# Later Down products, an earlier cast, and the first cuts of w2 on ScalarE and GpSimd

## The chip, the cores and the metric

The kernel runs on one core of a Trainium2 chip. The metric is the device time of one execution in microseconds. The engines are TensorE (PE; its weight loads are shown apart as PEld), VectorE (DVE), ScalarE (ACT), GpSimd (POOL) and SyncE (SP), which issues the transfers.

## The reference

The input x is 2048 tokens by 512, with 32 heads of 16 and an FFN of width 1792. All values are float32.

```python
xn = layernorm(x)
q, k, v = (xn @ wqkv) split in three, 32 heads
scores = q @ k.T * Dh**-0.5, masked to 0 <= i - j < 256
s = softmax(scores) @ v, heads joined, @ wo
h = silu(x @ w1) * (x @ w3)
g = silu(h @ w2)
out = x + s * g
```

Only the FFN's weights w1, w3 and w2 and its products are touched by the change.

## The kernel before, in words

The tokens are cut into four tiles of 512 (t = 0 to 3). Attention works on a tile in groups of heads; the FFN works on a tile in 14 blocks f of 128 columns of w1 and w3 (rows of w2). Everything is multiplied in float16 in two halves: a value is scaled by a power of two, its rounding to float16 is the upper half, what is left over is the lower half, and a product is three matmuls (upper times upper, upper times lower, lower times upper).

**Where the halves of a weight come from.** A weight block arrives as float32. Its squares are summed (`measure` at L249 for w1 and w3, `measure_down` at L941 for w2), the sums are cast to bfloat16 (`sb`, at L945 for w2), a tiny matmul (L285) adds them over partitions, and a chain of small VectorE instructions (L294 to L304, then L956 to L966) turns them into a scale `sw`. Then the block is cut. There are two ways to cut: `split` scales and rounds on ScalarE (L333) and subtracts on VectorE (L334); `split_pool` scales in place on ScalarE (L342), rounds on ScalarE (L343), and subtracts on GpSimd in four pieces of 128 columns (L345). w2 is measured and scaled in four groups of blocks, 0 to 3, 4 to 7, 8 to 10 and 11 to 13. Before the change group 0 is cut by `split`, the others by `split_pool`.

**The FFN.** `gate_up(t, f)` makes 24 matmuls into two PSUM banks (L1058): gate in one, up in the other. ScalarE takes the tanh of gate (L1073), VectorE forms the product out of the gate bank (L1077) and then the product with up (L1082), and so empties the banks; ScalarE casts the result (L1091) and GpSimd subtracts for the lower half (L339). There are two such banks, which take turns: whoever writes a bank next waits until its last reader is done. `down(t, k, b)` multiplies the blocks of group k with w2 for 128 tokens (L1283) into a bank of the same pair, and VectorE adds it to an accumulator (L1304 for group 0, L1307 for the others).

**Attention beside it.** For each unit of heads, a first pass writes scores (L671) into the tensor `s` or `po` and VectorE takes their maximum (L685); a second pass writes scores again (L759) into `s`, VectorE adds the mask (L766), ScalarE takes the exponential (L769), and L787 multiplies with the values into `po`. `s` has two buffers and `po` one. `project` is another user of the two banks (L601), with a ScalarE cast (L618) and a VectorE subtraction (L622). The turned x goes through `s` or `po` as well (L515), with L524 and L525 on VectorE.

**What sets the order.** TensorE's order is written out by hand: attention's steps take pieces from the list that `feed_forward` returns, so many matmuls per step. `later(n, work)` puts work off by n such steps. On the other engines a list scheduler orders by priority and by the estimated readiness; `urgent()` raises the priority, and `behind_exp()` or `tc.issue_after(...)` only fix that something is issued behind a given instruction.

Of the kernel before, what the change touches and what calls it, by code (L numbers as in the profile page):

```python
# [23 lines left out]
D = 512  # L24
# [59 lines left out]
def tile_block(ctx: ExitStack, tc: tile.TileContext, x, wqkv, wo, w1, w3, w2, out):  # L84
# [147 lines left out]
    def behind_exp():  # L232

        return tc.issue_after(lasts["exp"].ins) if "exp" in lasts else nullcontext()
# [97 lines left out]
    def split(hi, lo, raw, s):  # L332
        lasts["hi"] = nc.scalar.activation(hi, raw, AF.Copy, scale=s)  # L333
        lasts["cut"] = nc.vector.scalar_tensor_tensor(lo, raw, s, hi, op0=ALU.mult, op1=ALU.subtract)  # L334
# [6 lines left out]
    def split_pool(hi, lo, raw, s):  # L341
        nc.scalar.activation(raw, raw, AF.Copy, scale=s)  # L342
        nc.scalar.copy(hi, raw)  # L343
        for c in range(0, 512, P):
            nc.gpsimd.tensor_sub(lo[:, c:c + P], raw[:, c:c + P], hi[:, c:c + P])  # L345
# [587 lines left out]
    def measure_down(k, f):  # L933

        f0, f1 = GROUPS[k]
        n = f1 - f0
        if f == f0:
            NORMS[k] = small.tile([P, n], F32, name="ssq2")
        sq = ppool.tile([P, D], BF16, name="sqa", bufs=1)
        with behind_exp():  # L940
            nc.scalar.activation(sq, RAW2[f], AF.Square, accum_out=NORMS[k][:, f - f0:f - f0 + 1])  # L941
        if f < f1 - 1:
            return
        sb = small.tile([P, n], BF16, name="sb2")
        nc.vector.tensor_copy(sb, NORMS[k])  # L945

        def scale(s):
            p2 = small.tile([P, n], F32, name="pp2")
            def bound():
                with tc.issue_after(lasts["emptied"].ins):  # L950
                    rest(p2)
            return then(s, powers(sb, n, p2, None, s), lambda: later(1, bound))

        def rest(p2):
            assert measured >= set(range(f0, f1))
            nc.vector.tensor_mul(p2, p2, p13[:, f0:f1])  # L956
            q = small.tile([P, 1], F32, name="q")
            nc.vector.tensor_reduce(q, p2, axis=AX.X, op=ALU.max)
            nc.vector.tensor_scalar(down_scale[:, k:k + 1], q, 1.0 / (HS * WS), None, op0=ALU.mult)
            if k:  # L960
                nc.vector.tensor_max(fold_q, fold_q, q)
            else:
                nc.vector.tensor_copy(fold_q, q)
            nc.vector.reciprocal(q, q)
            sw = small.tile([P, 4], F32, name="sw2")
            nc.vector.tensor_scalar(sw[:, 0:n], p13[:, f0:f1], q, WS, op0=ALU.mult, op1=ALU.mult)  # L966

            def cut(f):
                raw = RAW2.pop(f)
                WF.setdefault((0, f), [[None, None], None])[1] = b = take(F16)  # L970
                if k == 0:
                    with tc.issue_after(lasts["emptied"].ins):
                        split(b[:, 0:D], b[:, D:], raw, sw[:, f - f0:f - f0 + 1])
                else:
                    with behind_exp():
                        split_pool(b[:, 0:D], b[:, D:], raw, sw[:, f - f0:f - f0 + 1])
                give(raw, after=5)
            for i, f in enumerate(range(f0, f1)):
                later(1 + 2 * i, lambda f=f: cut(f))
            if f1 == FB:  # L980
                later(4, fold_scales)
        beside_scores(2, scale)
# [394 lines left out]
    def feed_forward():  # L1377

        pieces = []
        late = []  # L1380
        cuts_at = []
        for t in range(NT):
            for f in range(FB):
                if t == 0:

                    if (f % 2 or f == 0) and f + LEAD < FB - 2:
                        pieces += [(0, lambda f=f: load(0, f)) for f in (range(f + LEAD, f + LEAD + 2) if f else range(4, LEAD + 1))]
                    elif f + LEAD == FB - 1:
                        pieces += [(0, lambda f=f: load(0, f)) for f in range(FB - 2, FB)]
                    if f % 2 and f + 3 < FB:  # L1390
                        pieces.append((0, lambda f=f + 3: later(8, lambda: measure(f, 1, 6)) if f == 6 else measure(f, 1)))
                    pieces += [(0, lambda f=f: load_down(0, f)) for f in range(f + 2 if f else 0, min(f + 3, FB))]
                    for m in range(f + 1 if f else 0, min(f + 2, FB)):
                        k = next(k for k, (_, f1) in enumerate(GROUPS) if m < f1)
                        pieces.append((0, lambda k=k, m=m: later(2, lambda: measure_down(k, m))))
                else:
                    if f == 0:
                        pieces += [(0, lambda t=t, f=f: load(t, f)) for f in range(2)]
                    if f + 2 < FB:
                        pieces.append((0, lambda t=t, f=f + 2: load(t, f)))  # L1400

                    if t == 1:
                        pieces.append((0, lambda t=t, f=f: load_down(t, f)))
                    if t == 1 and f in FOLD_AT:
                        work = fold_weights(FOLD_AT.index(f))
                        pieces.append((0, work[0]))
                        cuts_at.append((f + 2, work))
                    for at, work in cuts_at:
                        if t == 1 and f == at:
                            pieces.append((0, work[1]))  # L1410
                if f == FB - 4 and t + 2 < NT:
                    first, second = prepare_beside(t + 2, 8)
                    pieces += first
                if f == 0 and t > 2:
                    pieces += soon
                made = gate_up(t, f)
                for at, work in cuts_at:
                    if t == 1 and f == at:
                        made.insert(2, (0, lambda work=work: later(6, work[2])))
                pieces += made  # L1420
                pieces += late
                late = []
                if t < 2:
                    for k, (f0, f1) in enumerate(GROUPS):
                        if f == f1 - 1:
                            late = [q for b in range(4) for q in down(t, k, b)]
                for k, (j0, j1) in enumerate(FOLDS):
                    if t > 1 and f == 2 * j1 - 1:
                        soon, late = folds(t, k)
                        if k == 0 or t == NT - 1:  # L1430
                            pieces += soon
            if t + 2 < NT:
                pieces.append((0, second))
        return pieces + late
# [264 lines left out]
```

## Time and profile before

| | |
|---|---|
| median of three runs | 805.73 us (805.66 to 805.86) |
| the profiled execution | 805.44 us |
| its span | 803.7 us |
| TensorE busy | 791.4 us (98% of the span) |
| VectorE, ScalarE, GpSimd busy | 624.2, 393.0, 382.1 us |

The profile is taken from one execution. Busy times are of the whole span; a row of a timeline gives the start, the duration, the engine and line, the tile written and the tiles read, how many alike instructions were joined into the row, and in brackets for how long the engine had sat idle before it and whose work ended that. A bracket on TensorE is time in which no matmul was recorded as running. Rows named m are the two shared PSUM banks, s and po attention's, slot the shared SBUF buffers.

### The profile page before, as it was taken

Reading aid. Unit: us, or ns where it says so; the run is one execution under the profiler, and the core shown is the slowest. Engines: PE = TensorE matmul, PEld = TensorE weight load, DVE = VectorE, ACT = ScalarE, POOL = GpSimd, SP = SyncE. Lnnn points to the kernel's source line nnn. Section 1 sums busy time; section 2 is a strip of 40 time slices with the busy share of each in tenths; the row PEclk is TensorE's granted clock in tenths of the full one; section 3 lists DMA queues with packets and bytes.
Section 4 is the critical chain, followed back from the end, with each engine's and each line's share of the span. In section 5 each row is a group of like instructions: output and inputs, shape, how many; then the busy total and the mean of one; then the engine's idle time right before and its main releaser. Section 6 shows DMA issues by size and latency. Waiting matters only on the chain.

```text
span 803.7 us, 23972 instructions
## 1 busy us (share of the span) xinstructions
PE 791.4 (98%) x9181; PEld 404.3 (50%) x9181; DVE 624.2 (78%) x2005; ACT 393.0 (49%) x592; POOL 382.1 (48%) x746
## 2 busy tenths in 40 slices
PE   8999999999999999999999999999999999999997
PEld 4444444444554444444445444466544754466465
DVE  8887887888898678887888888777768876874537
ACT  6988685754455544345343344344444234444411
POOL 2355467552429445365443546330446276650770
PEclk9999999999999999999999999999999999999999
DMA  9887654836665564667555733665463553334431
GB/s 283 238 261 239 187 179 117 286 98 205 188 214 188 158 221 131 216 153 250 137 195 157 226 119 102 167 177 162 132 164 85 160 155 112 89 114 136 128 97 53
DMA packets 109858, 134.18 MB, mean 167 GB/s; under 512 B 18928, under 2 KB 64944, under 8 KB 109744
## 3 DMA queue, kind: packets, MB, share of 16 engines
q1 hardware_dynamic: 109456, 132.13, 55.3%
q8 instruction: 72, 1.18, 0.6%
q10 hardware_dynamic: 288, 0.52, 0.2%
q14 instruction: 42, 0.34, 0.1%
HBM read 91.23 MB, written 36.57 MB: 159 GB/s over the span
## 4 chain that ended last, share of the span: by engine, by line
PE 82%; DVE 6%; ACT 4%; DMA 3%; issue 2%; SPq 1%; POOL 0%; DVEq 0%; ACTq 0%; POOLq 0%
PE m L1058 30%; PE po L787 9%; PE m L601 9%; PE m L1283 8%; PE m L1201 7%; PE s L759 5%; PE m L1335 4%; PE m L567 4%; PE s L671 3%; PE po L671 2%; DVE junk L685 2%; ACT pt L769 1%; DMA dW<-slot 1%; ACT slot L342 1%; DVE s L766 1%
## 5 line engine op out<-in xcount | busy, mean ns | idle before, releaser
L1058 PE MATMUL m<-XH,slot 128*128 128x512 f16 x896 | 267.3, 380 | 1.2 <-DVE slot L622 0.8
L769 ACT ACTIVATE pt<-s,es 128x1024 f32<-128x1024 f32 x152 | 167.6, 1112 | 184.4 <-DVE s L766 180.4
L1058 PEld LDWEIGHTS <-slot 128*128 128x128 f16 x1344 | 125.0, 98 | 155.1 <-issue 12.5
L1058 PE MATMUL m<-XL,slot 128*128 128x512 f16 x448 | 169.8, 379 | 0.0
L766 DVE TENSOR_TENSOR s<-s,MK 128x256 f32<-128x256 f32 (+2 forms) x280 | 118.9, 435 | 53.6 <-PE s L759 48.2
L685 DVE CUSTOM_DVE_ANT_0 junk<-s,MW 128x320 bf16<-128x320 f32 x276 | 134.1, 486 | 18.7 <-PE s L671 10.6
L339 POOL TENSOR_TENSOR slot<-slot,slot 128x256 f16<-128x256 f32 (+1 forms) x86 | 57.6, 693 | 119.5 <-DVE slot L1339 54.3
L345 POOL TENSOR_TENSOR slot<-slot,slot 128x128 f16<-128x128 f32 x168 | 68.6, 442 | 73.5 <-ACT slot L343 68.2
L685 DVE CUSTOM_DVE_ANT_0 junk<-po,MW 128x320 bf16<-128x320 f32 x172 | 83.5, 486 | 5.3 <-DVE M L685 0.5
L1283 PE MATMUL m<-slot,slot 128*128 128x512 f16 x336 | 78.5, 380 | 0.3 <-DVE slot L1077 0.2
L787 PE MATMUL po<-pt,V 64*32 64x320 f32 (+4 forms) x2880 | 77.2, 342 | 0.8 <-DVE XL L525 0.8
L601 PE MATMUL m<-XH,slot 128*128 128x512 f16 x240 | 70.8, 380 | 0.4 <-DVE slot L1077 0.4
L1201 PE MATMUL m<-slot,slot 128*128 128x256 f16 x588 | 68.4, 273 | 0.1
L1073 ACT ACTIVATE slot<-m,sgs 128x512 f32<-128x512 f32 x56 | 38.3, 684 | 54.7 <-PE m L1058 54.1
L1116 POOL TENSOR_TENSOR slot<-slot,slot 128x256 f16<-128x256 f32 x98 | 64.5, 670 | 1.1
L787 PEld LDWEIGHTS po<-pt,V 64*32 64x32 f32 x2880 | 50.7, 106 | 22.6 <-PE s L515 0.9
L1201 PEld LDWEIGHTS <-slot 128*128 128x128 f16 x588 | 56.2, 98 | 11.6 <-issue 3.0
L1077 DVE SCALAR_TENSOR_TENSOR slot<-slot,m 128x512 f32<-128x512 f32 x56 | 38.3, 684 | 27.4 <-ACT slot L1073 27.4
L759 PE MATMUL s<-qa,KA 50*64 50x320 f16 (+3 forms) x1472 | 58.3, 259 | 0.1
L601 PEld LDWEIGHTS <-slot 128*128 128x128 f16 x392 | 36.5, 98 | 42.5 <-issue 1.9
L759 PEld LDWEIGHTS <-KA 50*64 50x64 f16 x1472 | 30.1, 105 | 51.9 <-issue 32.2
L1283 PEld LDWEIGHTS <-slot 128*128 128x128 f16 x336 | 30.7, 98 | 38.7 <-issue 4.3
(191 smaller groups left out, 1134.7 us busy)
## 6 DMA issues: line engine op xcount, KB each, us to landing
slot<-dW SPq DMA_DIRECT2D x98, 256.0 KB
slot<-in_B_w_dram SPq DMA_DIRECT2D x56, 256.0 KB
slot<-dFold SPq DMA_DIRECT2D x48, 256.0 KB
dW<-slot SPq DMA_DIRECT2D x42, 256.0 KB
slot<-in_A_x_dram SPq DMA_DIRECT2D x30, 256.0 KB
KA<-dK SPq DMA_DIRECT2D x24, 288.0 KB
slot<-dWQ SPq DMA_DIRECT2D x24, 256.0 KB
qa<-dQ SPq DMA_DIRECT2D x30, 192.0 KB
```

The source lines that it names most:

```text
L339: op(out[:, c], a[:, c], b[:, c])
L345: nc.gpsimd.tensor_sub(lo[:, c:c + P], raw[:, c:c + P], hi[:, c:c + P])
L601: nc.tensor.matmul(cell["pp"][:, cols[n]], w[:, (a * NC + c) * P:(a * NC + c + 1) * P], b[:, c, cols[n]], start=n == 0 and (c, i) == parts ...
L685: lasts["maximum"] = nc.vector.tensor_tensor_reduce(out=junk[:, :n], in0=s[:, r, :n], in1=mask, scale=1.0, scalar=NEG, op0=ALU.add, op1=AL ...
L759: nc.tensor.matmul(s[64 * h:64 * h + 64, r, o:o + 64 * n], ka[rows, 2 * p + a, 64 * (m + 4):64 * (m + 5)], qa[rows, 2 * p + a, 64 * (m + k ...
L766: nc.vector.tensor_add(v, v, MK[:, kind, of:of + n, :].unsqueeze(1).to_broadcast([P, 2 * len(which), n, 64]))
L769: lasts["exp"] = nc.scalar.activation(pt, s, AF.Exp, scale=es)
L787: nc.tensor.matmul(cell["po"][32 * i:32 * i + 32, h, 64 * (m + k):64 * (m + k + n)], V[64 * h:64 * h + 64, (4 * t + m // 2) % VB, hd * VW: ...
L1058: nc.tensor.matmul(cell[k], w[:, (a * NC + c) * P:(a * NC + c + 1) * P], b[:, c, :], start=c == 0 and i == 0, stop=c == NC - 1 and i == 2)
L1116: nc.gpsimd.tensor_sub(lo, view, hi)
L1201: nc.tensor.matmul(cell["ps"][:, c], made[:, f:f + P], wj[:, g:g + 256], start=j == j0 and c == 0 and n == 0, stop=j == j1 - 1 and n == 2, ...
L1283: nc.tensor.matmul(ps, hh[:, a * TW + b * P:a * TW + (b + 1) * P], w[:, c * D:(c + 1) * D], start=f == f0 and i == 0, stop=f == f1 - 1 and ...
```

## The change

Four edits, all in the first tile's FFN. The sums of a w2 group are cast at raised priority. Group 0 of w2 is cut like the other groups, with `split_pool`, and so leaves VectorE. The cuts of groups 0, 1 and 2 are four steps apart instead of two. And the Down products of groups 0, 1 and 2 of the first tile are put one FFN block later: group 0's came behind `gate_up(0, 4)`, and now come behind `gate_up(0, 5)`. The lines behind L945 carry other numbers in the changed kernel (L945 is L946, L1073 is L1070, L1077 is L1074, L1082 is L1079, L1091 is L1088, L1283 is L1280).

```diff
         sb = small.tile([P, n], BF16, name="sb2")
-        nc.vector.tensor_copy(sb, NORMS[k])
+        with urgent():
+            nc.vector.tensor_copy(sb, NORMS[k])
...
                 WF.setdefault((0, f), [[None, None], None])[1] = b = take(F16)
-                if k == 0:
-                    with tc.issue_after(lasts["emptied"].ins):
-                        split(b[:, 0:D], b[:, D:], raw, sw[:, f - f0:f - f0 + 1])
-                else:
-                    with behind_exp():
-                        split_pool(b[:, 0:D], b[:, D:], raw, sw[:, f - f0:f - f0 + 1])
+                with behind_exp():
+                    split_pool(b[:, 0:D], b[:, D:], raw, sw[:, f - f0:f - f0 + 1])
                 give(raw, after=5)
             for i, f in enumerate(range(f0, f1)):
-                later(1 + 2 * i, lambda f=f: cut(f))
+                later(1 + (4 if f1 < FB else 2) * i, lambda f=f: cut(f))
...
-        late = []
+        late, next_late = [], []
...
                 pieces += late
-                late = []
+                late, next_late = next_late, []
                 if t < 2:
                     for k, (f0, f1) in enumerate(GROUPS):
                         if f == f1 - 1:
-                            late = [q for b in range(4) for q in down(t, k, b)]
+                            products = [q for b in range(4) for q in down(t, k, b)]
+                            if t == 0 and f1 < FB:
+                                next_late = products
+                            else:
+                                late = late + products
```

Three places show how the instructions stand. On ScalarE, around the first Down products of the first tile (near 66 to 77 us of the profile before), before:

```order
L333 ACTIVATE slot_1325<-slot_807,sw_1178 128x512
L1091 CAST slot_1247<-slot_1170 128x512
L1073 ACTIVATE slot_1270<-m_1256,sgs 128x512
L941 ACTIVATE sqa,ssq_1159<-slot_1107 128x512
L249 ACTIVATE sqa,ssq<-slot_797 128x512
L249 ACTIVATE sqa,ssq<-slot_801 128x512
L769 ACTIVATE pt<-s,es_332 128x1024
```

and after, from the same exponential to the tanh of the next FFN block (L1070 is the tanh, L1088 the cast of h):

```order
L769 ACTIVATE pt<-s,es_332 128x1024
L249 ACTIVATE sqa,ssq<-slot_797 128x512
L342 ACTIVATE slot_711<-slot_711,sw_1178 128x512
L249 ACTIVATE sqa,ssq<-slot_801 128x512
L1088 CAST slot_1339<-slot_1271 128x512
L249 ACTIVATE sqa,ssq<-slot_798 128x512
L343 CAST slot_1365<-slot_711 128x512
L249 ACTIVATE sqa,ssq<-slot_802 128x512
L769 ACTIVATE pt<-s,es_332 128x1024
L1070 ACTIVATE slot_1420<-m_1357,sgs 128x512
```

The four L333 of group 0 stood in a row ahead of the fifth block's tanh; now each block of w2 has an L342 and an L343, spread among the squares, and the tanh shown last is the sixth block's, whose gate bank the first Down product takes.

On VectorE, where a projection and the turned x meet (near 118 to 120 us), before:

```order
L524 CAST XH<-po 128x2x128
L525 TENSOR_TENSOR XL<-po,XH 128x2x128
L622 SCALAR_TENSOR_TENSOR slot_2181<-m_2105,slot_2181 128x512
L834 RECIPROCAL dr<-dr 128x32
L766 TENSOR_TENSOR s<-s,MK 128x4x64
```

and after:

```order
L524 CAST XH<-po 128x2x128
L622 SCALAR_TENSOR_TENSOR slot_2194<-m_2123,slot_2194 128x512
L525 TENSOR_TENSOR XL<-po,XH 128x2x128
L834 RECIPROCAL dr<-dr 128x32
L766 TENSOR_TENSOR s<-s,MK 128x4x64
```

L622, which empties a bank, has moved ahead of L525, which empties `po`.

On VectorE a little later (near 125 us), before:

```order
L524 CAST XH<-po 128x2x128
L298 TENSOR_SCALAR al<-al 128x4
L525 TENSOR_TENSOR XL<-po,XH 128x2x128
L1082 SCALAR_TENSOR_TENSOR slot_2208<-m_2269,slot_2208 128x512
L302 TENSOR_SCALAR pi<-al 128x4
```

and after:

```order
L524 CAST XH<-po 128x2x128
L946 CAST sb_2400<-ssq_2022 128x3
L298 TENSOR_SCALAR al<-al 128x4
L525 TENSOR_TENSOR XL<-po,XH 128x2x128
L1079 SCALAR_TENSOR_TENSOR slot_2219<-m_2278,slot_2219 128x512
```

The cast of the third w2 group's sums (L946) now stands ahead of L525. The order is the same from about 205 us to the end on every engine.

## The prediction

> **What bounds the kernel now.** I read the busy times first, then the span cut into stretches, then TensorE's timeline with its waits, and last the timelines of the engines that those waits name.
>
> ```profile
> span 803.7 us, 23972 instructions
> PE 791.4 (98%) x9181; PEld 404.3 (50%) x9181; DVE 624.2 (78%) x2005; ACT 393.0 (49%) x592; POOL 382.1 (48%) x746
> 66.00:102.00 36.00, 34.22 (x364) 15.87 (x368) 29.86 (x111) 25.93 (x51) 13.58 (x34) 1.00 0.71 219
> 102.00:127.00 25.00, 22.32 (x307) 11.27 (x298) 20.30 (x77) 20.40 (x41) 17.26 (x45) 1.00 0.56 175
> 127.00:205.00 78.00, 78.00 (x888) 37.36 (x873) 65.19 (x234) 45.06 (x70) 39.93 (x100) 1.00 0.55 175
> 205.00:780.00 575.00, 574.08 (x7098) 296.71 (x7097) 437.26 (x1337) 244.23 (x320) 278.46 (x484) 1.00 0.53 156
> ```
>
> The stretches give the busy time of TensorE, its weight loads, VectorE, ScalarE and GpSimd, then the granted clock (1.00), the DMA share and GB/s. TensorE is busy 791.4 of 803.7 us, and from 127 to 780 us it misses 0.9 us in all. The change adds no matmul and takes none away, so it can only act through TensorE's waits, and the written order differs between 67 and 205 us alone. What can be won lies in 66 to 102 us (36.00 − 34.22 = 1.78 idle) and 102 to 127 us (25.00 − 22.32 = 2.68 idle). These are the waits there:
>
> ```profile
> 70.06 0.38 PE L1058 MATMUL m<-XL,slot 128*128 128x512 f16 x1
> 70.69 1.46 PE L1283 MATMUL m<-slot,slot 128*128 128x512 f16 x6 [0.25 <-DVE slot L1077]
> 72.24 0.42 PE L759 MATMUL s<-qa,KA 50*64 50x320 f16 x10
> 73.08 0.33 PE L671 MATMUL s<-KA,qa 48*64 48x320 f16 x4 [0.43 <-ACT pt L769]
> 73.89 0.33 PE L671 MATMUL po<-KA,qa 48*64 48x320 f16 x4 [0.47 <-DVE M L685]
> 74.15 5.35 PE L1283 MATMUL m<-slot,slot 128*128 128x512 f16 x24
> 79.70 2.06 PE L787 MATMUL po<-pt,V 64*32 64x320 f32 x72
> 100.88 0.20 PE L285 MATMUL s<-sb,onesb 64*64 64x4 bf16 x4 [0.33 <-DVE sb L945]
> 111.23 0.59 PE L601 MATMUL m<-XH,slot 128*128 128x512 f16 x2 [0.43 <-DVE slot L1077]
> 113.76 0.30 PE L671 MATMUL s<-KA,qa 48*64 48x256 f16 x4 [0.73 <-ACT pt L769]
> 119.98 0.59 PE L1058 MATMUL m<-XH,slot 128*128 128x512 f16 x2 [0.43 <-DVE slot L622]
> 124.48 0.33 PE L671 MATMUL s<-KA,qa 48*64 48x320 f16 x4 [0.22 <-DVE al L295]
> 125.83 2.04 PE L787 MATMUL po<-pt,V 64*32 64x320 f32 x72 [0.79 <-DVE XL L525]
> ```
>
> Start and duration, then in brackets the idle time and who ended it. The nine brackets sum to 4.08. A matmul in a stream advances every (5.35 − 0.38)/23 = 0.216 us, though the record of one lasts 0.38, so 0.17 of each wait is hidden under the record ahead: 4.08 + 9 × 0.17 = 5.6 us are really lost. No version that only moves work here can win more than about that.
>
> **The first Down products (three waits, 0.25, 0.43 and 0.47).** They stand behind ScalarE's queue:
>
> ```profile
> 64.75 0.72 ACT L333 ACTIVATE slot<-slot,sw 128x512 f16<-128x512 f32 x1
> 65.36 0.61 ACT L343 CAST slot<-slot 128x512 f16<-128x512 f32 x1
> 65.86 1.12 ACT L769 ACTIVATE pt<-s,es 128x1024 f32<-128x1024 f32 x1
> 66.87 1.95 ACT L333 ACTIVATE slot<-slot,sw 128x512 f16<-128x512 f32 x3
> 68.71 0.62 ACT L1091 CAST slot<-slot 128x512 f16<-128x512 f32 x1
> 69.22 0.70 ACT L1073 ACTIVATE slot<-m,sgs 128x512 f32<-128x512 f32 x1
> 71.31 0.63 ACT L249 ACTIVATE sqa<-slot 128x512 bf16<-128x512 f32 x1
> 71.94 1.09 ACT L769 ACTIVATE pt<-s,es 128x1024 f32<-128x1024 f32 x1
> ```
>
> The tanh of the fifth FFN block (L1073) waits behind three scalings of w2 (66.87 to 68.71, 1.84 us); its product on VectorE empties the bank that the first Down product writes. After the change no scaling stands there: behind the exponential come one cast L343 (0.50 from start to start), the h cast (0.51), and the tanh, at 66.87 + 0.50 + 0.51 = 67.88 instead of 69.22. The first Down products now stand one block later. So the three waits of 0.25 + 0.43 + 0.47 + 3 × 0.17 = 1.7 us go.
>
> What is late next is the sixth block's tanh. In the new order twelve instructions stand between the two tanhs: two L342 and two L343 (the second and third cut of w2), five squares (one L941, four L249), one h cast and two exponentials. By start-to-start times, as the engine ran them back to back: L342 0.62 twice, L343 0.50 twice, L941 0.61, L249 0.63 four times, h cast 0.51, exponential 1.01 twice, in all 7.9 us. With the tanh's own 0.58, the next one starts at 67.88 + 0.58 + 7.9 = 76.36. From tanh to the first Down matmul it was 70.69 − 69.22 = 1.47, so Down starts at 77.8. TensorE itself is there at 70.06 + 0.21 (end of the fifth block) + 24 × 0.216 for the sixth + 0.7 for the scores between (72.24 to 73.08 before, less what they waited) = 76.1. A new wait of **1.7 us** takes the place of the old 1.7: this part is worth nothing.
>
> **The cuts: what each engine gets.** Four cuts lose one L333 each and get L342 and L343: by the rows above about +0.5 us each, +2.0 us on ScalarE. VectorE loses four L334 of 0.78 (3.1 us), GpSimd gets sixteen L345:
>
> ```profile
> L334 DVE SCALAR_TENSOR_TENSOR slot<-slot,sw,slot 128x512 f16<-128x512 f32 x4 | 3.1, 784 | 0.1
> L345 POOL TENSOR_TENSOR slot<-slot,slot 128x128 f16<-128x128 f32 x168 | 68.6, 442 | 73.5 <-ACT slot L343 68.2 <-DMA slot<-in_B_w_dram 1.9 <-DMA qa<-mt 1.8
> ```
>
> That is 16 × 0.44 = 7.0 us for an engine that is busy 13.58 of 36 us here. With four steps between cuts the last pair (L342, L343) stands behind the sixth tanh with two squares: 76.36 + 0.58 + 2 × 0.63 + 0.62 + 0.50 = 79.3, the cast itself 0.61 long, and 4 × 0.44 behind it end near 81.6. The Down matmuls ahead of its reader (six, then the value products of 2.06, then three and one more) put that reader at 77.8 + 6 × 0.216 + 0.3 + 2.06 + 0.65 = 82.1: hidden, by half a microsecond; each 0.1 beyond that costs 0.1.
>
> ScalarE is where the two microseconds can hurt. The next batch of exponentials and the tanh behind it:
>
> ```profile
> 84.79 1.11 ACT L769 ACTIVATE pt<-s,es 128x1024 f32<-128x1024 f32 x1 [7.51 <-DVE s L766]
> 89.80 1.11 ACT L769 ACTIVATE pt<-s,es 128x1024 f32<-128x1024 f32 x1
> 109.78 0.67 ACT L1073 ACTIVATE slot<-m,sgs 128x512 f32<-128x512 f32 x1
> 112.60 1.11 ACT L769 ACTIVATE pt<-s,es 128x1024 f32<-128x1024 f32 x1
> 118.60 0.60 ACT L618 ACTIVATE slot<-m 128x512 f16<-128x512 f32 x1
> 119.23 0.69 DVE L622 SCALAR_TENSOR_TENSOR slot<-m,slot 128x512 f16<-128x512 f32 x1 [0.96 <-ACT slot L618]
> 125.14 0.16 DVE L298 TENSOR_SCALAR al<-al 128x4 int32<-128x4 int32 x1
> 125.26 0.42 DVE L525 TENSOR_TENSOR XL<-po,XH 128x256 f16<-128x256 f32 x1
> ```
>
> Ahead of 84.79 ScalarE sat idle 7.51 us, so the extra 2.0 us are absorbed there. Between 84.79 and 89.80 (5.01) the same instructions stand as before; started by the same mask, the second exponential ends near 90.8, and TensorE wants that scores buffer back near 90.6, since the Down products no longer lie in between: a new wait, between 0.1 and 0.5, I take **0.3**.
>
> **The urgent cast (wait of 0.33).** Before, the cast of w2's sums (L945) is the eleventh of a row of small VectorE instructions. Urgent, it goes ahead of them and waits only for its square. The wait of 0.33 + 0.17 = 0.5 goes to 0.
>
> **102 to 127 us (five waits).** *Output projection L601* (0.43 + 0.17 = 0.6): the product it waits for stands behind the small chain, and seven small instructions fall away ahead of it; such a one holds VectorE 0.12 us (125.14 to 125.26), together 0.85; TensorE comes 0.6 earlier. Half stays: **0.3**. *Scores L671 after the exponential* (0.73 + 0.17 = 0.9): from tanh 109.78 to exponential 112.60 it is 2.82, one cast fewer stands between, 2.3; what stays is **0.5** with TensorE's own earlier arrival counted. *Gate L1058 behind L622* (0.6): ScalarE's L618 comes earlier as its queue is shorter, but the subtraction L525 of the turned x now stands behind L622 on VectorE, and the next scores into po wait for it: **0.3**. *al L295 and XL L525* (0.4 and 1.0): the second group's Down products, which stood right ahead, are now one block later, and TensorE has a gate_up block there instead. Both go to **0**, with about 0.4 us to spare, as one cast (L946 of the changed kernel, waiting for a square on ScalarE) now stands ahead of L525.
>
> **Sum.** Before 5.6; after 1.7 + 0.3 + 0.3 + 0.5 + 0.3 = 3.1. Gain 2.5 us. The profiled execution took 805.44 with a span of 803.7; the median of the runs is 805.73, 0.3 above it, so the forecast is 805.73 − 2.5 = **803.2 us**. The ends of the open terms (first Down 1.0 to 2.5, scores 0.1 to 0.5, the other three together 0.5 to 2.0) give 801.7 to 804.7 as this case's own range.
>
> **A price that no row of before shows** is what GpSimd's sixteen subtractions do to VectorE beside them. The nearest rows:
>
> ```profile
> 61.83 0.49 DVE L966 TENSOR_SCALAR sw<-p,q 128x4 f32<-128x4 f32 x1
> 110.29 0.23 DVE L966 TENSOR_SCALAR sw<-p,q 128x4 f32<-128x4 f32 x1
> 59.94 3.13 POOL L345 TENSOR_TENSOR slot<-slot,slot 128x128 f16<-128x128 f32 x8 [1.87 <-DMA slot<-in_B_w_dram]
> ```
>
> The same tiny instruction took 0.49 beside a run of L345 on GpSimd and 0.23 in the second place, so 0.26 is the most that one such meeting has cost, and none is the least. In my walk the new subtractions lie beside VectorE's mask and maximum work, which reads PSUM, and meet one instruction that reads SBUF alone; that is off the path, and I take 0. The Trainium skill (SBUF — State Buffer, section "SBUF: two separate sides") states that GpSimd and VectorE share a port pair as an exclusive lock, so that the loser blocks for the whole instruction, for a VectorE instruction with two SBUF inputs or in its two-port mode. The two rows agree with it as far as they go; by it the sum would stay, unless the subtractions slide beside the small chain, which is the fourth rival.
>
> **The rivals.** A difference under 0.2% (1.6 us) can't be told from none here. *(1) The forecast*, 803.2: chance 0.50. *(2) All waits go*: the new waits at the first Down and behind the exponentials don't come up, since VectorE's lost 3.1 us pull more forward than I count. 805.73 − 5.6 = 800.1. For it speaks GpSimd's and ScalarE's idle time; against it the ten instructions between the tanhs. Chance 0.10. *(3) The other side: ScalarE's queue becomes the limit.* from 64.75 to 71.94 its rows follow one another without a gap, and 2.0 us more stand there. If this moves the tanhs and exponentials late by d beyond my walk at each of the five waits that stay, the time is 803.2 + 5d: no gain from d = 0.5, slower by 0.2% from d = 0.82; at d = 1.0 it is 808.2. For it: ScalarE is busy 25.93 of 36 us there. Against it: the 7.51 us ahead of 84.79, which empty the queue. Chance 0.16, most of it slower. *(4) The ports:* ten small instructions from the power-of-two chain to L966, each late by 0.26, are 2.6 us, which would eat the gain: 805.8. Chance 0.06. *(5) The waits only change place:* the other open terms stay at their old size, as the first Down does, and the time is that of before, 805.7. Chance 0.18: the order is written out, and a wait removed lets TensorE run into the next.
>
> **How the numbers follow.** Faster by over 0.2%: 0.48 from the forecast and 0.10 from (2), 0.58. Within: 0.02, 0.18, 0.06 and 0.03 of (3), 0.29. Slower: 0.13. The range goes from 800.8, between (2) and the forecast's lower end, to 807.0, in the middle of (3); outside lie about 0.07 below and 0.13 above.
>
> **What would show it.** Right: TensorE's waits at L1283 near 70.7 and at the two scores behind it gone, one of about 1.5 (bracket) at the first Down near 78, named L1074 of the changed kernel; none at the sums' matmul near 100; none at the value products near 125; TensorE idle 66 to 127 us near 2.2 instead of 4.46. Wrong: an idle of ScalarE ahead of the tanhs (then the queue isn't what is late), the fourth cut's subtraction named at a Down matmul, or waits later than 205 us, which this reading says can't change by more than their 0.9.

## The result, and the profile after

The changed kernel takes 804.0 us (median of 14 executions, 803.54 to 804.84) against 805.72 before (805.26 to 806.05): a ratio of 0.998, with a 95% interval of 0.9972 to 0.9987. It is 1.7 us faster, with 1.0 and 2.3 as the ends of the interval. The forecast was a gain of 2.5 us. The profiled execution took 803.54 us with a span of 801.4. It ran at the lower end of the 14, as the one of before did, so the two profiles differ by 1.9 us.

The page of the changed kernel and its stretches (columns as before):

```profile
span 801.4 us, 23995 instructions
PE 791.6 (99%) x9181; PEld 404.0 (50%) x9181; DVE 620.4 (77%) x2001; ACT 395.5 (49%) x596; POOL 387.6 (48%) x762
66.00:102.00 36.00, 34.21 (x384) 16.02 (x385) 27.67 (x106) 31.95 (x63) 24.45 (x64) 1.00 0.72 227
102.00:127.00 25.00, 24.07 (x326) 11.86 (x313) 23.04 (x86) 19.41 (x40) 13.61 (x34) 1.00 0.56 173
127.00:205.00 78.00, 77.69 (x859) 37.24 (x852) 63.75 (x235) 43.49 (x63) 39.58 (x100) 1.00 0.55 176
```

TensorE's work is the same (791.6 against 791.4). From 66 to 102 us it idles as long as before (1.79 against 1.78), though ScalarE is now busy 31.95 us there and GpSimd 24.45. The gain is in 102 to 127 us: 0.93 idle instead of 2.68. From 127 to 205, where nothing was missing before, 0.31 are missing now.

All waits of TensorE from 60 to 210 us in the changed kernel:

```profile
77.78 1.46 PE L1280 MATMUL m<-slot,slot 128*128 128x512 f16 x6 [1.44 <-DVE slot L1074]
91.22 0.30 PE L671 MATMUL s<-KA,qa 48*64 48x256 f16 x4 [0.35 <-ACT pt L769]
110.77 0.59 PE L601 MATMUL m<-XH,slot 128*128 128x512 f16 x2 [0.53 <-DVE slot L1074]
112.86 0.30 PE L671 MATMUL s<-KA,qa 48*64 48x256 f16 x4 [0.28 <-ACT pt L769]
146.13 0.59 PE L1055 MATMUL m<-XH,slot 128*128 128x512 f16 x2 [0.19 <-DVE slot L1304]
```

Counted as before (bracket plus 0.17 hidden under the record ahead), they cost 1.61, 0.52, 0.70, 0.45 and 0.36, together 3.64 us against 5.6 before: 1.96 less. That this is close to the 1.9 between the two profiled executions is partly luck. The prediction's nine waits of before leave out a tenth, the first row below; with it before counts 5.98 and the difference 2.34. How much TensorE really gained can be read from the distance between two rows that both kernels have: from the scores matmul that starts at 58.11 before and 58.12 after to the first value projection (L567), which is the second row before and the last row after.

```profile
96.24 0.59 PE L1058 MATMUL m<-XH,slot 128*128 128x512 f16 x2 [0.20 <-DVE slot L622]
204.16 0.39 PE L567 MATMUL m<-wvh,XH 128*128 128x512 f16 x1
```

```profile
202.29 0.39 PE L567 MATMUL m<-wvh,XH 128*128 128x512 f16 x1
```

That is 146.05 against 144.17 us, so 1.88 us were gained. The brackets alone differ by 4.28 − 2.79 = 1.49, and there are five fewer of them, so 0.17 for each, taken from a stream of 128x512 matmuls, is too much: 0.08 on the average would fit. The waits tell where the time went; their sums are good to about half a microsecond.

ScalarE in the changed kernel, the rows that the forecast walked to: the tanhs of the fifth and the sixth block, and the two exponentials of the next scores.

```profile
67.90 0.69 ACT L1070 ACTIVATE slot<-m,sgs 128x512 f32<-128x512 f32 x1
76.32 0.68 ACT L1070 ACTIVATE slot<-m,sgs 128x512 f32<-128x512 f32 x1
85.05 1.11 ACT L769 ACTIVATE pt<-s,es 128x1024 f32<-128x1024 f32 x1 [3.19 <-DVE s L766]
90.06 1.11 ACT L769 ACTIVATE pt<-s,es 128x1024 f32<-128x1024 f32 x1
```

The forecast had the tanhs at 67.88 and 76.36 and the first Down matmul at 77.8. They came at 67.90, 76.32 and 77.78.

### The profile page after: what moved, and what is told of

It reads as the page before. It is cut to its first block, busy times and chain, and to the rows that moved or that the text cites. A ratio compares the mean times of both kernels' runs of the same rounds, so it can differ in the third digit from the quotient of the medians.

```text
span 801.4 us, 23995 instructions
## 1 busy us (share of the span) xinstructions
PE 791.6 (99%) x9181; PEld 404.0 (50%) x9181; DVE 620.4 (77%) x2001; ACT 395.5 (49%) x596; POOL 387.6 (48%) x762
## 4 chain that ended last, share of the span: by engine, by line
PE 81%; DVE 6%; DMA 5%; ACT 3%; SPq 3%; issue 1%; POOL 1%; DVEq 0%; ACTq 0%; POOLq 0%
PE m L1055 31%; PE po L787 9%; PE m L601 8%; PE m L1198 8%; PE m L1280 7%; PE s L759 5%; PE m L1332 4%; PE m L567 4%; PE s L671 3%; DMA slot<-in_B_w_dram 2%; PE po L671 2%; DVE junk L685 1%; POOL slot L345 1%; DMA KA<-dK 1%; SPq L880 1%
## 5 line engine op out<-in xcount | busy, mean ns | idle before, releaser
L345 POOL TENSOR_TENSOR slot<-slot,slot 128x128 f16<-128x128 f32 x184 | 74.9, 441 | 77.8 <-ACT slot L343 51.3
L1280 PE MATMUL m<-slot,slot 128*128 128x512 f16 x336 | 78.5, 380 | 1.4 <-DVE slot L1074 1.4
L601 PE MATMUL m<-XH,slot 128*128 128x512 f16 x240 | 70.8, 380 | 0.5 <-DVE slot L1074 0.5
L1070 ACT ACTIVATE slot<-m,sgs 128x512 f32<-128x512 f32 x56 | 38.3, 685 | 60.4 <-PE m L1055 60.3
L1074 DVE SCALAR_TENSOR_TENSOR slot<-slot,m 128x512 f32<-128x512 f32 x56 | 38.3, 684 | 28.4 <-ACT slot L1070 27.9
L601 PEld LDWEIGHTS <-slot 128*128 128x128 f16 x392 | 36.5, 98 | 42.6 <-issue 1.8
L1280 PEld LDWEIGHTS <-slot 128*128 128x128 f16 x336 | 30.8, 98 | 39.5 <-issue 5.1
```

Of the source, the lines that this page charges most:

```text
L601: nc.tensor.matmul(cell["pp"][:, cols[n]], w[:, (a * NC + c) * P:(a * NC + c + 1) * P], b[:, c, cols[n]], start=n == 0 and (c, i) == parts ...
L1280: nc.tensor.matmul(ps, hh[:, a * TW + b * P:a * TW + (b + 1) * P], w[:, c * D:(c + 1) * D], start=f == f0 and i == 0, stop=f == f1 - 1 and ...
```

## The experiments

Two theories stood against each other. The first, the walk of the prediction: every part of the change acts through ScalarE's queue and the two banks, the new wait at the first Down products is ScalarE's instructions between two tanhs, and each edit has its share. The rival: one edit carries all of the gain (the later Down products, or VectorE's relief by GpSimd), and the rest is idle work. Each time below stands beside the median of the kernel before on the same chip. "The walk" is the prediction's way of following each engine's instructions one by one.

### The cut by ScalarE and GpSimd alone

```diff
-                if k == 0:
-                    with tc.issue_after(lasts["emptied"].ins):
-                        split(b[:, 0:D], b[:, D:], raw, sw[:, f - f0:f - f0 + 1])
-                else:
-                    with behind_exp():
-                        split_pool(b[:, 0:D], b[:, D:], raw, sw[:, f - f0:f - f0 + 1])
+                with behind_exp():
+                    split_pool(b[:, 0:D], b[:, D:], raw, sw[:, f - f0:f - f0 + 1])
```

> The cut by ScalarE and GpSimd alone (group 0 of w2 by split_pool, two steps apart as before; Down products at their old place, cast of the sums not urgent). The walk: the last block's two ScalarE instructions stand behind a square, an exponential and two more squares, so its lower half leaves GpSimd near 77.1 us while the Down matmul that reads it is due near 73.4; 3.7 us of new wait less about 1.5 of the old ones: 807.9, slower by 2.2. Rival (VectorE's relief is the gain): VectorE loses 3.1 us and the three waits of 1.7 go, 804.0 to 804.5. Rival (cover is enough): 805.7.

Measured: 808.31 against 805.53, ratio 1.0029 (1.0018 to 1.0040), 2.8 us slower. TensorE's waits in the first Down products, where their weights are late:

```profile
72.24 0.59 PE L1279 MATMUL m<-slot,slot 128*128 128x512 f16 x2 [0.51 <-POOL slot L345]
75.07 0.38 PE L1279 MATMUL m<-slot,slot 128*128 128x512 f16 x1 [0.69 <-ACT slot L343]
76.73 6.16 PE L1279 MATMUL m<-slot,slot 128*128 128x512 f16 x20 [1.28 <-POOL slot L345]
```

The last lower half is there at 76.7 (77.1 was expected), and the products stand still for it. But this is less than half of the 2.8 us. Counted as above, the waits of this kernel up to 205 us cost 1.1 us more than those of before. The rest is TensorE's clock, which was granted at 0.72 and 0.50 in the two stretches behind the pauses (columns as before):

```profile
76.00:78.00 2.00, 1.27 (x4) 0.55 (x4) 0.34 (x1) 2.00 (x5) 1.93 (x4) 0.72 0.98 339
78.00:80.00 2.00, 2.00 (x7) 0.63 (x5) 0.90 (x4) 1.11 (x4) 0.00 (x0) 0.50 0.98 261
```

The 20 matmuls at 76.73 took 6.16 us; at 0.216 each they take 19 × 0.216 + 0.38 = 4.5, so the clock cost about 1.7 us. Five of the seven executions have a mean clock of 0.998 and took 808.3 to 808.8 us; the other two, at 1.000, took 806.6 and 806.8, which is 1.1 to 1.3 over before. The waits alone therefore cost 1.1 to 1.3 us, less than the 2.2 of the walk, which came near the measured time by luck. Why the clock fell is not shown. The dip comes behind two pauses close together (0.69 and 1.28), while a single one of 1.91, in the changed kernel with two steps between the cuts, has none behind it; no other profile here has such a dip between 20 and 210 us.

In the old place, then, the cut by GpSimd makes the weights late, and VectorE's relief doesn't make up for it.

### The later Down products alone, and with the distance

```diff
-                            late = [q for b in range(4) for q in down(t, k, b)]
+                            products = [q for b in range(4) for q in down(t, k, b)]
+                            if t == 0 and f1 < FB:
+                                next_late = products
+                            else:
+                                late = late + products
```

> The later Down products alone (cut by split on VectorE, cast not urgent). The walk: the fifth block's tanh stays at 69.22, so the three waits near 70.7 to 73.9 (1.7 in all) stay, with gate_up in Down's place; the sixth tanh comes near 77.1, a wait of 0.8 at the first Down; the waits at 124.5 and 125.8 (1.4) go. 805.2. Rival (later Down is the whole gain): 804.0. Rival (the new place costs what the old did): 805.7.

Measured: 805.04 against 805.53, ratio 0.9991 (0.9981 to 1.0000): 0.5 us by the medians, as the walk had it, and not the whole gain (1.5 us at the interval's end). A second kernel adds the four steps between the cuts, and nothing else:

```diff
-                later(1 + 2 * i, lambda f=f: cut(f))
+                later(1 + (4 if f1 < FB else 2) * i, lambda f=f: cut(f))
```

> The later Down products with the four-step distance of the cuts, and nothing else (split on VectorE, cast not urgent). The theory as it stands after the first eight runs (later Down and the distance need each other and carry the gain; the cut by GpSimd and the urgent cast give nothing): 803.9, as the changed kernel. Rival (the urgent cast counts once the Down products are later): 804.4. Rival (without GpSimd's cut the distance is worth nothing, as with the later Down products alone): 805.0.

Measured: 804.31 against 805.68, ratio 0.9980 (0.9971 to 0.9989). That is the changed kernel's ratio, without GpSimd's cut and without the urgent cast. The time lies nearer to the first rival's 804.4 than to the 803.9 of the theory. But this kernel's trace has no wait at the sums' matmul that an urgent cast could take away, and the kernel below that has the urgent cast beside the same `split` is no shorter between the two rows used above (144.78 against 144.44 us). First the waits of the later Down products alone from 60 to 130 us, then those of the same kernel with the distance:

```profile
71.02 0.59 PE L1058 MATMUL m<-XH,slot 128*128 128x512 f16 x2 [0.24 <-DVE slot L1077]
73.42 0.33 PE L671 MATMUL s<-KA,qa 48*64 48x320 f16 x4 [0.43 <-ACT pt L769]
74.22 0.33 PE L671 MATMUL po<-KA,qa 48*64 48x320 f16 x4 [0.47 <-DVE M L685]
78.97 1.45 PE L1283 MATMUL m<-slot,slot 128*128 128x512 f16 x6 [0.43 <-DVE slot L1077]
111.38 0.59 PE L601 MATMUL m<-XH,slot 128*128 128x512 f16 x2 [0.47 <-DVE slot L1077]
114.07 0.30 PE L671 MATMUL s<-KA,qa 48*64 48x256 f16 x4 [0.90 <-ACT pt L769]
120.01 0.33 PE L671 MATMUL po<-KA,qa 48*64 48x320 f16 x4 [0.55 <-DVE XL L525]
```

```profile
70.71 0.59 PE L1058 MATMUL m<-XH,slot 128*128 128x512 f16 x2 [0.24 <-DVE slot L1077]
73.11 0.33 PE L671 MATMUL s<-KA,qa 48*64 48x320 f16 x4 [0.59 <-ACT pt L769]
78.66 1.46 PE L1283 MATMUL m<-slot,slot 128*128 128x512 f16 x6 [1.09 <-DVE slot L1077]
111.08 0.59 PE L601 MATMUL m<-XH,slot 128*128 128x512 f16 x2 [0.47 <-DVE slot L1077]
113.17 0.30 PE L671 MATMUL s<-KA,qa 48*64 48x256 f16 x4 [0.29 <-ACT pt L769]
```

Near 71 to 79 us both lose the same (brackets 1.57 and 1.92, with 0.17 for each wait 2.3 and 2.4), which is a little more than the changed kernel's 1.61 + 0.52. Near 113 and 120 us the distance takes 0.90 to 0.29 and 0.55 to nothing; a wait of 0.18 near 146 comes with it.

### The changed kernel with the cut by split, twice

The edit gives group 0 its `split` back and leaves the other three edits:

```diff
-                with behind_exp():
-                    split_pool(b[:, 0:D], b[:, D:], raw, sw[:, f - f0:f - f0 + 1])
+                if k == 0:
+                    with tc.issue_after(lasts["emptied"].ins):
+                        split(b[:, 0:D], b[:, D:], raw, sw[:, f - f0:f - f0 + 1])
+                else:
+                    with behind_exp():
+                        split_pool(b[:, 0:D], b[:, D:], raw, sw[:, f - f0:f - f0 + 1])
```

> The changed kernel with group 0 still cut by split. The walk: as later_only without the 0.5 of the cast, 804.7; the wait at the first Down is 0.8 instead of 1.6, and the three waits near 70.7 to 73.9 are back with 1.7. Rival (ScalarE's 2.0 us more are what the new wait is made of, and nothing else): the wait at the first Down falls by 1 us and nothing comes back, 803.0. Rival (later Down is the whole gain): 804.0.

Measured: 803.71 against 805.53, ratio 0.9979 (0.9970 to 0.9988), a microsecond better than the walk. The same kernel once more, beside the changed kernel:

> The changed kernel with group 0 cut by split, once more, as its first profile fell on its slowest execution (start-up 1.1 us late). The walk: the waits near 71 to 79 sum to 2.4 us against 2.1 in the changed kernel, so it is 0.3 to 0.5 slower than the changed kernel in the same call, 804.3. Rival (ScalarE's extra 2.0 us are the loss): 0.5 or more faster than the changed kernel, under 803.5.

> The changed kernel once more, beside the others of this call. Both theories: 804.0; its profile shows the waits of the first profile (1.44 at the first Down, 0.35, 0.53 and 0.28 behind it) and another start of the first scores matmul of the second pass, as the start-up differs between executions.

Measured side by side: 803.96 with `split` (803.75 to 804.29), 803.88 for the changed kernel (803.52 to 804.52). The two are not told apart. The waits are 0.25, 0.60 and 1.10 near 71 to 79 in place of one of 1.44 and one of 0.35, so the profile has the walk's 0.3 us between them there. Near 147 us the wait is 0.53 against 0.20, and over the whole stretch from the scores near 58 to L567 it is 144.78 against 144.23 us. The times don't confirm it: if GpSimd's cut gains anything, it is under what they can tell. The walk's 804.7 for this kernel took 0.5 off for the cast, which gives nothing by itself, and nothing for what the distance does near 113 and 120 us.

### The distance, in two steps

> The changed kernel with the cuts two steps apart as before. The walk: two more of the cuts' instructions stand ahead of the fifth tanh (69.0 instead of 67.9) and the sixth tanh comes near 77.5, the first Down matmul near 79.0 where TensorE stands ready at 76.3: a wait of 2.7 and one of 0.2, 1.3 more than the changed kernel, 805.3. Rival (the distance doesn't matter): 804.0.

Measured: 804.99 against 805.53, ratio 0.9995 (0.9985 to 1.0004). With two steps the changed kernel is hardly faster than before, 0.5 us by the medians. The walk put all of that at the first Down products. There the brackets are 1.91 and 0.22, less than it expected, and two more stand near 114 and 120 (0.90 and 0.55). Then four steps for group 0 alone:

```diff
-                later(1 + (4 if f1 < FB else 2) * i, lambda f=f: cut(f))
+                later(1 + (4 if k == 0 else 2) * i, lambda f=f: cut(f))
```

> The changed kernel with four steps between the cuts of group 0 alone, two between those of groups 1 and 2. Theory (the distance acts in two places: at the first Down products through group 0, 0.6 us, and at the exponential near 113 and the turned x near 120 through group 1, 0.8 less 0.4 that comes back near 146): the first Down waits 1.6 as in the changed kernel, the scores near 113 wait 1.1 instead of 0.5, 804.4. Rival (all of it is group 0): 803.9. Rival (all of it is group 1): 805.0.

Measured: 804.54 against 805.68, ratio 0.9987 (0.9978 to 0.9996). The waits at the first Down and behind it are those of the changed kernel (1.44, 0.35), and these two, which the distance of groups 1 and 2 had taken away, are back:

```profile
113.70 0.30 PE L671 MATMUL s<-KA,qa 48*64 48x256 f16 x4 [0.90 <-ACT pt L769]
119.64 0.33 PE L671 MATMUL po<-KA,qa 48*64 48x320 f16 x4 [0.55 <-DVE XL L525]
```

By the medians, of the 1.1 us that the distance brings (from 0.5 to 1.6 under the kernel before) 0.6 are group 0's and 0.5 those of groups 1 and 2; the intervals are as wide as these steps, so the split rests on the waits more than on the times. Groups 1 and 2 were not told apart. The distance with the old place of the Down products wasn't tried, so that the distance needs the later place is argued and not shown.

### The urgent cast alone

```diff
-        nc.vector.tensor_copy(sb, NORMS[k])
+        with urgent():
+            nc.vector.tensor_copy(sb, NORMS[k])
```

> The kernel before with the urgent cast alone. The walk: the wait of 0.5 at the sums' matmul near 100.9 goes and the next one gains nothing from it: 805.2. Rival: TensorE runs into the wait behind it, 805.7.

Measured: 805.72 against 805.51, ratio 1.0003 (0.9994 to 1.0012): no gain. TensorE, VectorE and ScalarE with this edit alone:

```profile
100.94 0.20 PE L285 MATMUL s<-sb,onesb 64*64 64x4 bf16 x4 [0.26 <-DVE sb L946]
100.73 0.16 DVE L946 CAST sb<-ssq 128x4 bf16<-128x4 f32 x1
99.64 0.62 ACT L941 ACTIVATE sqa<-slot 128x512 bf16<-128x512 f32 x1
```

and ScalarE and VectorE in the changed kernel:

```profile
96.85 0.62 ACT L941 ACTIVATE sqa<-slot 128x512 bf16<-128x512 f32 x1
97.72 0.16 DVE L946 CAST sb<-ssq 128x4 bf16<-128x4 f32 x1
```

With the urgent cast alone the wait falls from 0.33 to 0.26, and the next one, at L601, grows from 0.43 to 0.58. The cast moved by one place only in VectorE's row of small instructions (ahead of L448), and starts 0.38 us after its square's sum was read out (100.35). In the changed kernel the wait is gone because the square runs 2.8 us earlier on ScalarE. In the kernel with the later Down products alone the cast stands at 98.93, with no urgency and no wait.

### Two squares out of the way of the sixth tanh

Whether the new wait at the first Down products is made of ScalarE's queue between two tanhs, this kernel tests: two squares go to VectorE and four are issued later, so that three ScalarE squares stand between the tanhs instead of five.

```diff
+        def tied(i, raw):
+            with behind_exp():
+                one(i, raw)
         for i, raw in enumerate(parts):
-            if apart:
+            if i in put_off:
+                later(apart * (i + 1) + (2 if len(put_off) == 4 else 2), lambda i=i, raw=raw: tied(i, raw))
+            elif apart:
                 later(apart * (i + 1), lambda i=i, raw=raw: one(i, raw))
...
-            later(apart * len(parts) + 2, behind_bank)
+            later(apart * len(parts) + 2 + (2 if len(put_off) == 4 else 0) * bool(put_off), behind_bank)
...
-        sb = squares([raws[0][0], raws[1][0], raws[0][1], raws[1][1]], on_act=4 if f > 2 else 2, apart=apart)
+        sb = squares([raws[0][0], raws[1][0], raws[0][1], raws[1][1]], on_act=2 if f in (0, 2, 6) else 4, apart=apart,
+                     put_off={6: (2, 3), 8: (0, 1, 2, 3)}.get(f, ()))
```

> The changed kernel with two squares (of w1 and w3, blocks 6 and 7) put on VectorE behind its maxima, and the four of blocks 8 and 9 put behind the sixth tanh: two ScalarE squares fewer between the fifth and the sixth tanh. The walk: 2 x 0.63 us earlier, so the wait at the first Down falls from 1.6 to about 0.35 and nothing comes in its place: 802.7, 1.25 faster than the changed kernel. Rival (the wait only changes place): the sums' matmul near 79 or the scores wait instead, 804.0. Rival (VectorE becomes late): slower than the changed kernel.

Measured: 803.07 (802.89 to 803.88) against 805.51, ratio 0.9968 (0.9956 to 0.9979); 0.8 below the changed kernel beside it (803.88). The wait at the first Down, and the one that came up behind it, with VectorE's rows ahead of the cast that ends it:

```profile
76.59 1.46 PE L1286 MATMUL m<-slot,slot 128*128 128x512 f16 x6 [0.22 <-DVE slot L1080]
82.94 0.20 PE L290 MATMUL s<-sb,onesb 64*64 64x4 bf16 x4 [0.85 <-DVE sb L266]
81.73 0.75 DVE L1307 TENSOR_SCALAR slot<-m,dsc 128x512 f32<-128x512 f32 x1
82.73 0.16 DVE L266 CAST sb<-ssq 128x4 bf16<-128x4 f32 x1
```

From 1.44 to 0.22: ScalarE's queue between the tanhs is the cause of this wait, to a tenth of a microsecond of the walk (0.39 lost against 0.35 expected). The time confirms less of it, since waits came in its place: the 0.85 near 82.9, 0.23 near 141, and 0.60 instead of 0.19 near 146. In this profiled execution they took back all of the gain (144.33 us between the two rows, against 144.23); its 803.47 is 0.4 above the median, and the median has 0.8 of the 1.25 expected. The wait near 82.9 is the edit's own: it issued the cast of blocks 8 and 9 two steps later, behind a Down accumulation. Issued where it was:

```diff
-            later(apart * len(parts) + 2 + (2 if len(put_off) == 4 else 0) * bool(put_off), behind_bank)
+            later(apart * len(parts) + 2, behind_bank)
```

> The kernel with the moved squares, with the cast of the sums of blocks 8 and 9 issued two steps earlier, ahead of the copies of the attention output and the Down accumulation on VectorE. Theory: the wait of 0.85 (0.5 lost) at the sums' matmul near 82.9 goes, 802.6; the exponential near 89 can take 0.2 of it back. Rival (the exponential near 90 or the scores behind it wait the same): 803.1.

Measured: 803.26 (802.86 to 804.45) against 805.68, ratio 0.9969 (0.9958 to 0.9981). The wait near 82.9 is gone, the one at the first Down stays at 0.21, and part of the gain is taken back near 90:

```profile
90.05 0.30 PE L676 MATMUL s<-KA,qa 48*64 48x256 f16 x4 [0.42 <-ACT pt L774]
```

Its profiled execution, 802.86, is the fastest of all (143.05 us between the two rows); by the medians, each of six executions, it can't be told from the one ahead of it. A last kernel also put off the cuts of blocks 8 and 9 of w1 and w3, to free the exponential near 89:

```diff
-                        later((1, 5, 9, 13)[2 * i + k], lambda i=i, k=k: tied(i, k))
+                        later((1, 5, 9, 13)[2 * i + k] + (2 if f == 8 else 0), lambda i=i, k=k: tied(i, k))
```

> The same with the cuts of blocks 8 and 9 of w1 and w3 two steps later, so that one scaling and one cast fewer stand ahead of the second exponential behind the first Down products. Theory: that exponential comes 0.5 earlier and the scores behind it don't wait: 802.3, unless the later cuts make GpSimd late (then a wait at a gate_up near 118 or at its store): 802.6 or more.

Measured: 803.90 (803.58 to 804.63) against 805.68, ratio 0.9976 (0.9966 to 0.9985): no gain, and by the medians 0.6 slower than the kernel ahead of it. On ScalarE the two exponentials:

```profile
84.69 1.11 ACT L774 ACTIVATE pt<-s,es 128x1024 f32<-128x1024 f32 x1 [3.26 <-DVE s L771]
89.70 1.11 ACT L774 ACTIVATE pt<-s,es 128x1024 f32<-128x1024 f32 x1
```

The distance is 5.01 us as before, with four scalings and three casts of w1 and w3 between them in both kernels. So others took the place of the two that were put off; the trace doesn't name their blocks. Why the kernel is slower was not followed up; its waits near 111 and 113 (0.74 and 0.41 against 0.54 and 0.29) and near 147 (0.56 against 0.20) are longer.

## Why the prediction was right, and where not

The forecast of 803.2 is 0.8 below the median; the time lies in the range given and the sign is right. The signs that it named came true: the waits near 70.7 to 73.9 and at the sums' matmul and the value products are gone, the one at the first Down is 1.44, and TensorE idles 2.72 us from 66 to 127 us (near 2.2 was named, 4.46 before). By its own steps:

- **Only waits can move.** Held: TensorE's busy time is the same, and what changed lies between 66 and 205 us. The count of them was off in two ways that partly cancel, as said above: the wait of 0.20 near 96 is missing from its 5.6, and 0.17 for each wait is too much.
- **The first Down products, "worth nothing".** Held: three waits of 1.7 went, one of 1.61 came, within 0.04 us of the place named. The run with two squares fewer between the tanhs shows the cause, where the profile only suggested it. (Twelve instructions stand between them, as the walk counts; the "ten" in its rivals is a slip.)
- **The scores near 90.6, 0.3.** Came to 0.52, just above the bound of 0.5. The exponential that starts the five microseconds began 0.26 later than before instead of at the same time.
- **The urgent cast, 0.5 to 0.** The size was right and the cause wrong: alone, the raised priority moved the cast by one place and not to the front of its row, and gave nothing. The wait went with the square, which runs earlier on ScalarE with the later Down products, urgent or not.
- **L601 behind the product, 0.6 to 0.3.** Failed: 0.70. VectorE has no recorded idle time from the first row below to the small chain, and that row waits for GpSimd (L474). Before:

```profile
103.65 0.63 DVE L477 TENSOR_SCALAR slot<-slot,mv,rs 128x512 f32<-128x512 f32 x1 [1.12 <-POOL rs L474]
110.48 0.69 DVE L1077 SCALAR_TENSOR_TENSOR slot<-slot,m 128x512 f32<-128x512 f32 x1
```

  and after:

```profile
103.05 0.63 DVE L477 TENSOR_SCALAR slot<-slot,mv,rs 128x512 f32<-128x512 f32 x1 [0.44 <-POOL rs L474]
109.33 0.67 ACT L1070 ACTIVATE slot<-m,sgs 128x512 f32<-128x512 f32 x1
109.69 0.23 DVE L967 TENSOR_SCALAR sw<-p,q 128x4 f32<-128x4 f32 x1
110.03 0.69 DVE L1074 SCALAR_TENSOR_TENSOR slot<-slot,m 128x512 f32<-128x512 f32 x1
```

  The end of the chain comes 0.60 earlier (L967 at 109.69, L966 at 110.29 before), as GpSimd's rs does. TensorE is ready 0.55 earlier (its last matmul ahead starts at 109.87 against 110.42), so the chain gains next to nothing on it. The small instructions that fell away ahead of L448, which GpSimd's part waits for, gave 0.28 and not 0.85: from the last maximum to L448 it is 0.70 us before (99.89 to 100.59) and 0.42 after (99.57 to 99.99). And the product itself comes only 0.45 earlier, since the tanh does: it now ends last, at 110.00 against 109.92 for the chain, so a shorter chain alone could win nothing more.
- **L671 behind the exponential, 0.5.** Came to 0.45, and the run with four steps for group 0 alone shows that the distance between the cuts of groups 1 and 2 makes it: without it, 1.07. **L1058 behind L622, 0.3.** Came to nothing; the wait for XL that it was to leave stands near 120 (0.55) in the kernels without that distance. **al and XL, 0.** Held.
- **Not in the sum: 0.36 near 146**, where the second group's Down accumulation now stands among the turned x on VectorE. The prediction had no term behind 127 us, where nothing was missing before.

Of the 0.55 us by which the waits after exceed the 3.1 forecast, 0.4 is L601, 0.2 the scores near 91 and 0.36 the wait near 146, less 0.09 on the first Down, 0.05 on L671 and 0.3 on L1058. The rest, from the 1.96 that these sums leave to the measured 1.7, is within the spread of the executions and within what the count of the waits is good for.

Of the rivals, the third (ScalarE's queue becomes the limit) did not come: the tanhs stand where the walk had them, and the idle 7.51 us ahead of 84.79 took the added work up, with 3.19 of them left (the row at 85.05 in the changed kernel waits so long for the mask). The fourth, GpSimd against VectorE, did not come either where it was feared: from the start of L298 to the end of L966 the small chain takes 2.96 us before and 2.95 after. The second (all waits go) and the fifth (they only change place) did not come; the fifth is what the changed kernel with two steps between the cuts comes close to.

## What to carry to other kernels

When the engine that sets the time waits, ask what starts the chain in front of the wait, and follow it one engine further before giving it a price: here the row of small instructions waited for GpSimd, and the product behind it for the tanh as well. A cast made urgent is not thereby first in its row, and it is no earlier than its input. Brackets show where time is lost; how much was gained is safer read between two rows that both kernels have. And an edit that only makes sense beside another (a slower cut beside a later reader) has to be measured alone as well: here the later place and the wider distance carry the gain, and the cut that they made room for gives nothing that the times can tell.

## What was not expected of the hardware

**GpSimd and VectorE beside each other.** With the two squares on VectorE (two SBUF inputs, the same block twice), a group of four subtractions on GpSimd that lay beside them took 2.49 us. The next group, beside maxima that read PSUM, took 1.60. In rows of the kernel with the moved squares:

```profile
74.82 0.82 DVE L251 CUSTOM_DVE_ANT_0 junk<-slot 128x512 bf16<-128x512 f32 x1
76.45 0.80 DVE L251 CUSTOM_DVE_ANT_0 junk<-slot 128x512 bf16<-128x512 f32 x1
75.04 2.49 POOL L350 TENSOR_TENSOR slot<-slot,slot 128x128 f16<-128x128 f32 x4
78.23 1.60 POOL L350 TENSOR_TENSOR slot<-slot,slot 128x128 f16<-128x128 f32 x4 [0.70 <-ACT slot L348]
```

Each square took 0.80 to 0.82 against a median of 0.688 over all twelve of that kernel. The Trainium skill (SBUF — State Buffer, section "SBUF: two separate sides") says that the two engines share a port pair as a lock, which the loser waits for through a whole instruction. These rows agree with it in direction: GpSimd lost 0.89 beside 1.62 us of squares. It is one meeting only, and it cost nothing here, as no wait of TensorE names GpSimd.

**The start.** Up to about 65 us every engine's instructions are in the same order in the changed kernel and in the one with `split`, and yet the scores matmul near 58 started at different times in two profiled executions, first of the changed kernel and then of the first run with `split`:

```profile
58.12 0.41 PE L759 MATMUL s<-qa,KA 50*64 50x320 f16 x10
```

```profile
59.25 0.41 PE L759 MATMUL s<-qa,KA 50*64 50x320 f16 x10
```

That 1.13 us is as large as most effects compared here, and its cause was not followed up. So single profiles were compared by their waits behind that point, and times by medians.
